# Attention and mixture of experts in one kernel: the first slot's token list on GpSimd's queue, ranks in the scores' PSUM, turns ahead of copies, the second slot turned by TensorE

## The chip, the cores and the metric

The kernel runs on one core of a Trainium2 chip. The metric is device time in microseconds (us) of one execution, the median of three runs. One more execution is recorded by the hardware profiler; its rows give the durations, and its own time stands beside its span in the table below. PE is TensorE (the matmul array), DVE VectorE, ACT ScalarE, POOL GpSimd, SP SyncE, which here only starts transfers.

## The reference

Two stages. A chunked attention (8 batches, 8 heads, 576 positions, head size 64; softmax inside each chunk of 64 positions), whose output, seen as 4608 rows of 512, goes through a mixture of experts in which each row uses one of 8 experts:

```python
scores = scale * np.matmul(q_c, k_c.transpose(0, 1, 2, 4, 3))
attn = softmax(scores)                       # within a chunk of 64
x = np.matmul(attn, v_c)                     # -> rows [4608, 512]

logits = x @ w_gate + modality_bias[modality_id]
e_idx = np.argmax(logits, axis=1)
gate_w = softmax(logits)[row, e_idx]
for e in range(8):
    mask = e_idx == e
    h = np.maximum(x[mask] @ w1[e], 0.0)     # 512 -> 1024
    out[mask] = gate_w[mask, None] * (h @ w2[e])
```

Which expert a row takes is known only when its attention is done. All is in float32; the kernel splits the operands of the expert matmuls in a high and a low part (three matmuls for one).

## The kernel before

**Attention in rounds.** A tile is 128 rows, and a round takes two; 18 rounds make the 36 tiles. In round r the code issues: `evict(r-1)` (ACT copies the attention output, L280), `parts(r-2)` (ACT copies the gate logits out of PSUM, L299) and `put(r-2)` (rows to DRAM tensor `xd`, on ACT's queue, L305), `scores(r+1)` (64 small matmuls into PSUM tile `sb`, L232; DVE takes the maxima, L235, and subtracts, L236), `transposes(r)` (PE, L257; ACT copies, L259), `rows(2r-2)`, `rows(2r-1)` (matmuls that turn the output back and form the logits, into the PSUM pairs `y0`, `y1`, L289; DVE scales, L291), `exps(r+1)` (ACT's exponential, L242; a half-sum on GpSimd, L244), `sums(r)` (DVE, L248), `values(r)` (L272). Each engine runs its own instructions strictly in the order in which the code issues them. The first 12 rounds (`NPURE`) are pure; the steps of the last six are strewn by `merge` between the matmuls of the first expert slots, where one `pair()` of PSUM holds both halves of a step.

**Routing.** Tiles form groups: `GROUPS = ((0, 8), (8, 8), (16, 20))` (first tile, count). When a group's logits are there, `route` runs as a generator, one step per `advance`: logits and argmax on GpSimd and DVE, running counts (`scan`), then two small matmuls that give each row its rank within its expert (L364, L365), taken out by DVE (L366 to L374). `scatter` then writes one 64-byte record (row number, gate) per row into a DRAM table `tab`, in which every expert has its own stretch: one indirect transfer of GpSimd's queue per tile (L380). In the pure rounds the ranks use `pairs[0]`, where `rows` writes as well.

**Slots.** A slot is 384 rows of one expert (the last two 256). Slot 0 is chosen by `early_table(0)` after group 0, slots 1 to 3 by `early_table(1)` after group 1, the others by `slot_table` after group 2. Since a list's end may be unwritten, `blank` (SP, L439) writes 384 records of a number out of range behind each of the chosen lists, or, before slot 4, behind the rows of each of the 8 experts. `locate` (SP, L559) reads a list into `tl`; it waits for the scatters and the blanks. `gather` (GpSimd) copies the row numbers (`tk`, L576 or L578) and fetches the rows into `xg` by three indirect transfers (L580). Slot 0's rows are turned by PE (`split`, L620 to L623); later slots' rows go to DRAM (`stash`), come back in blocks of 32 (`place`), are turned in blocks on DVE (`turn`, L606) and split in two parts (`part`, L611, L612).

**A slot's matmuls.** Eight steps f: `first` (12 matmuls, L679, then relu on ACT, L683, and the low part on DVE, L684), and one step later `second` (9 matmuls, L693). Weights come by `fetch` (SP, two steps' worth, 1 MB, L638) into three buffers `raw`; ACT copies the high part (L649) and DVE the low one (L653).

**What sets the order.** Two tables written by hand. `PLAN` gives, for round r and place k in it (`hook(r, k)`), what else is issued: fetches, list, gather, weight splits (`hi`, `lo`) of slot 0. `PREP` gives the same for slot s and step f; `settle` drains all open routing steps. SP's queue is in order too: a transfer that waits holds all transfers behind it.

Of the kernel before, what the change touches and what calls it, by code (L numbers as in the profile page):

```python
# [89 lines left out]
def attention_moe(ctx: ExitStack, tc: tile.TileContext, qkv, mod, cst, bias, wcat, wfst, out):  # L90
# [160 lines left out]
    def transposes(r, banks):  # L251
        ex = exs.pop(r)
        ats = []
        for j, bank in enumerate(banks):
            ap = bank.rearrange("p (k q) -> p k q", k=NP)
            for k in range(NP):
                PE.transpose(ap[:, k, :], ex[:, j * NP + k].rearrange("p u k -> p (u k)"), ident)  # L257
# [1 line left out]
            A.copy(ats[j], ap)  # L259
# [681 lines left out]
```

## Time and profile before

| | |
|---|---|
| median of 3 runs | 592.32 us (592.18 to 596.98) |
| the profiled execution | 592.26 us; its span, first to last instruction, 590.1 us |
| PE busy | 537.2 us, 91% of the span; mean granted clock 0.963 |
| DVE, ACT, POOL busy | 358.0, 240.8, 167.5 us |
| moved by DMA | 131.16 MB, mean 222 GB/s |
| first matmul of slot 0, 1, 2 | 102.94, 170.18, 220.25 us |

Busy time counts the engine's executing time; in the 40-slice strips of the page each digit is the busy share of a 14.75 us slice in tenths. A row of the timeline reads: start, duration, engine, line, operation, tiles and shapes, count; in brackets the idle time of the engine just before, and who ended it. "PEclk" is the share of full TensorE clock that was granted. Rows of SPq and ACTq are starts of transfers.

### The profile page before, as it was taken

What the parts mean: (1) busy time and instruction counts of PE and PEld (TensorE: products, weight loads), DVE (VectorE), ACT (ScalarE), POOL (GpSimd) and SP (SyncE); (2) the same over time, 40 slices, a digit from 0 to 9 for tenths busy, and PEclk for the clock granted to TensorE, in tenths of its full rate; (3) what the DMA queues carried; (4) which work ended last, traced back from release to release, by engine and by line L of the source; (5) the groups of instructions that cost most, each with busy time, mean ns of one, the idle gap of its engine ahead of it and who ended that gap; (6) DMA issues with size and microseconds to landing.
All of it is one profiled execution on the core that took longest, in us unless ns stands there. A gap on an engine that the chain in (4) does not pass through costs nothing.

```text
span 590.1 us, 12218 instructions
## 1 busy us (share of the span) xinstructions
PE 537.2 (91%) x4901; PEld 477.8 (81%) x4902; DVE 358.0 (61%) x608; ACT 240.8 (41%) x402; POOL 167.5 (28%) x171
## 2 busy tenths in 40 slices
PE   6878877996999999998699999999999999999993
PEld 3767876875877889996599998999998988998993
DVE  4659767873576597961455656555564656465741
ACT  3546354533344444431343434343443434435531
POOL 2313646113313237724222230404022110302001
PEclk9989787998899999998799999999999999999998
DMA  8989789758777727207997584867667474756500
GB/s 345 401 301 341 246 301 347 292 192 264 194 243 251 228 94 253 77 18 241 311 284 269 156 278 150 289 197 253 204 186 283 120 261 154 249 179 190 186 37 25
DMA packets 55073, 131.16 MB, mean 222 GB/s; under 512 B 11806, under 2 KB 29918, under 8 KB 46048
## 3 DMA queue, kind: packets, MB, share of 16 engines
q1 hardware_dynamic: 43040, 101.68, 52.5%
q0 software_dynamic: 7072, 19.18, 9.3%
q10 hardware_dynamic: 4896, 9.44, 4.1%
q8 instruction: 40, 0.66, 0.4%
q14 instruction: 25, 0.20, 0.1%
HBM read 102.16 MB, written 28.64 MB: 222 GB/s over the span
## 4 chain that ended last, share of the span: by engine, by line
PE 59%; issue 19%; DVE 9%; DMA 4%; ACT 3%; POOL 3%; SPq 1%; ACTq 0%; POOLq 0%; DVEq 0%
PE y L679 21%; PE sb L693 16%; PE t L693 8%; PE y L289 5%; PE t L679 3%; PE t L272 2%; PE sb L232 1%; DVE mx L235 1%; PE t L257 1%; POOL out L708 1%; DVE xr L291 1%; DVE wl L653 1%; DMA raw<-in_wfst 1%; DMA qk<-in_qkv 1%; POOL xg L580 1%
## 5 line engine op out<-in xcount | busy, mean ns | idle before, releaser
L653 DVE TENSOR_TENSOR wl<-raw,wh 128x1024 fp32r<-128x1024 f32 x104 | 127.4, 1227 | 59.4 <-ACT wh L649 59.3
L679 PE MATMUL y<-xh,wh 128*128 128x384 f32 (+1 forms) x364 | 119.6, 329 | 0.0
L679 PE MATMUL y<-xl,wh 128*128 128x384 f32 (+1 forms) x364 | 119.4, 328 | 0.0
L679 PE MATMUL y<-xh,wl 128*128 128x384 f32 (+1 forms) x364 | 119.0, 327 | 0.0
L649 ACT CAST wh<-raw 128x1024 fp32r<-128x1024 f32 x104 | 108.1, 1042 | 26.1 <-DMA raw<-in_wcat 22.1
L683 ACT ACTIVATE hh<-y 128x384 fp32r<-128x384 f32 (+1 forms) x91 | 43.1, 473 | 171.7 <-PE y L679 171.4
L684 DVE SCALAR_TENSOR_TENSOR hl<-y,hh 128x384 fp32r<-128x384 f32 (+1 forms) x91 | 48.4, 532 | 96.4 <-ACT hh L683 96.4
L708 POOL DMA_INDIRECT out<-yo,tk x37 | 39.8, 1077 | 228.0 <-DVE yo L707 199.7
L693 PE MATMUL sb<-wh,hl 128*128 128x512 f32 x208 | 84.5, 406 | 6.4 <-DVE hl L684 6.4
L693 PE MATMUL sb<-wh,hh 128*128 128x512 f32 x208 | 84.4, 406 | 1.7 <-ACT hh L683 1.7
L693 PE MATMUL sb<-wl,hh 128*128 128x512 f32 x208 | 83.1, 399 | 0.0
L679 PEld LDWEIGHTS y<-xh,wh 128*128 128x128 f32 x364 | 68.9, 189 | 3.7
L679 PEld LDWEIGHTS y<-xl,wh 128*128 128x128 f32 x364 | 68.9, 189 | 3.5
L679 PEld LDWEIGHTS y<-xh,wl 128*128 128x128 f32 x364 | 68.7, 189 | 0.0
L693 PEld LDWEIGHTS sb<-wh,hl 128*128 128x128 f32 x208 | 39.8, 192 | 17.2 <-DVE hl L684 7.8
L289 PE MATMUL y<-cs,xt 128*128 128x144 f32 x288 | 45.1, 316 | 6.5 <-DVE ra L369 5.4
L289 PEld LDWEIGHTS y<-cs,xt 128*128 128x128 f32 x288 | 42.9, 217 | 6.8 <-DVE ra L369 5.9
L244 POOL TENSOR_TENSOR sr<-ex 128x512 f32<-128x512 f32 x18 | 23.7, 1319 | 86.7 <-ACT ex L242 86.6
L580 POOL DMA_INDIRECT xg<-xd,tk x37 | 44.2, 1193 | 13.9 <-issue 7.3
L693 PEld LDWEIGHTS sb<-wh,hh 128*128 128x128 f32 x208 | 39.6, 191 | 7.5 <-ACT hh L683 2.0
L380 POOL DMA_INDIRECT tab<-tg,pi x36 | 39.3, 1091 | 20.5 <-DVE pi L374 10.9
L693 PEld LDWEIGHTS sb<-wl,hh 128*128 128x128 f32 x208 | 39.7, 191 | 5.7
(178 smaller groups left out, 707.5 us busy)
## 6 DMA issues: line engine op xcount, KB each, us to landing
raw<-in_wcat SPq DMA_DIRECT2D x48, 1024.0 KB, 6.3
qk<-in_qkv SPq DMA_DIRECT2D x18, 1024.0 KB, 7.9
v<-in_qkv SPq DMA_DIRECT2D x18, 512.0 KB, 5.9
xd<-xr ACTq DMA_DIRECT2D x18, 512.0 KB, 6.6
xs<-xg SPq DMA_DIRECT2D x10, 768.0 KB, 5.7
xq<-xs SPq DMA_DIRECT2D x40, 192.0 KB, 4.3
raw<-in_wfst SPq DMA_DIRECT2D x4, 1024.0 KB, 9.5
xs<-xg SPq DMA_DIRECT2D x2, 512.0 KB, 6.9
```

The source lines that it names most:

```text
L244: G.tensor_tensor(sring[r % 2][:, :, :, 0:32], exu[:, :, :, 0:32], exu[:, :, :, 32:64], ALU.add)
L272: PE.matmul(xps[u][hh * 64:hh * 64 + 64, p, cs_], v[us, h, c], ats[h // NP][us, h % NP, cs_], start=True, stop=True)
L289: PE.matmul(fp[:, p, 0:GWC], xt[:, p, :], gw[:, p, :], start=True, stop=True)
L380: w = G.indirect_dma_start(tab, bass.IndirectOffsetOnAxis(ap=pi[:, j:j + 1], axis=0), tg[:, j, :], None, bounds_check=E * CAP - 1, oob_is_ ...
L580: G.indirect_dma_start(xg[:, t, :], None, xd[0:n, :], bass.IndirectOffsetOnAxis(ap=tk[:, t:t + 1], axis=0), bounds_check=n - 1, oob_is_err ...
L649: A.copy(hi, raw)
L653: (G if pool else V).tensor_tensor(lo, raw, hi.bitcast(F32), ALU.subtract)
L679: PE.matmul(hp, a[:, ks], b[:, k, 0:n], start=(m == 0), stop=(m == 3 * NK - 1))
L683: A.activation(hh[:, 0:n], hp, AF.Relu)
L684: V.scalar_tensor_tensor(hl[:, 0:n], hp, 0.0, hh.bitcast(F32)[:, 0:n], ALU.max, ALU.subtract)
L693: PE.matmul(y, a[:, tsl], b[:, DM:2 * DM], start=(f == 0 and i == 0), stop=(f == NF - 1 and i == 2))
L708: w = G.indirect_dma_start(out, bass.IndirectOffsetOnAxis(ap=tk[:, t:t + 1], axis=0), yo, None, bounds_check=N - 1, oob_is_err=False)
```

## The change

- **Order of a round.** `parts` and `put` of round r-1 are issued in round r after `exps(r+1)`, instead of those of r-2 at its start; `hook(r, 1)` stands ahead of `sums(r)`.
- **Ranks.** In the pure rounds they are put into `sb[:, 0]` at place 1 of a round, after `rows`, instead of `pairs[0]` at place 0. `GATES` holds group 1's routing back to round 10 and its ranks to round 11 or later.
- **Turns ahead of copies.** `transposes` issues all eight turns, then the two copies.
- **First list.** `setup` blanks the first 384 records of each expert's stretch of `tab` once, in one transfer of ACT's queue with 1024 pieces of 192 bytes. `blank 0` goes away; `early_table(0)` no longer works out an end, and has one step less per slot. `locate 0` is issued by GpSimd, on its own queue, at round 8.
- **Weights of slot 0.** `fetch 0` moves to the start of round 8; the low parts of its first two steps are formed on GpSimd (`lop`) at rounds 10 and 11 instead of on DVE (`lo`).
- **Second slot.** Its rows are turned by PE (`split 1 0`, `split 1 2` at steps 6 and 7 of slot 0), so its weights come in the other row order (`wfst`); `stash 1`, `place 1`, `turn 1`, `part 1` go away.
- **Late tiles.** The last 20 tiles form two groups of 12 and 8. After the ranks of the last one the ends of the experts' rows are cast to `stop`, and the eight blanks before slot 4 are issued there, ahead of `slot_table`; `PREP` no longer has `blank 2`.

On GpSimd in the pure rounds: `tab` is a scatter, `sr` the half-sum of a round, `tl` slot 0's list, `xg` its rows, `lp` and `lh` routing of group 1. Before:

```order
L380 DMA tab<-tg_130,pi_1037 41472x16 x2
L320 TENSOR_TENSOR lp_140<-lp_140,ris 128x512
L244 TENSOR_TENSOR sr_142<-ex 128x16x32
L325 TENSOR_TENSOR lh<-lp_140 128x256
L326 TENSOR_TENSOR lh<-lh 128x8x16
L327 TENSOR_TENSOR lg<-lh 128x64
L328 TENSOR_TENSOR lg<-lg,mb 128x64
L244 TENSOR_TENSOR sr_143<-ex 128x16x32
L576 COPY tk_164<-tl_163 128x3
L580 DMA xg<-xd,tk_164 128x512 x3
```

The same place after the change:

```order
L394 DMA tab<-tg_131,pi_964 41472x16 x3
L247 TENSOR_TENSOR sr_147<-ex 128x16x32
L575 TENSOR_LOAD e_tab_1078
L575 ISA x2
L576 ISA
L576 DMA tl_168<-tab 128x3x2
L593 COPY tk_169<-tl_168 128x3
L597 DMA xg<-xd,tk_169 128x512 x3
L247 TENSOR_TENSOR sr_146<-ex 128x16x32
L327 TENSOR_TENSOR lp_144<-lp_144,ris 128x512
```

The list's transfer has come into GpSimd's own queue behind the last three scatters and one half-sum; the half-sum of round 10 (`sr_146`) now stands behind the list and the gather, and group 1's routing behind that.

On GpSimd in slot 0, around the second slot's gather (`tl` with its list, `tk`). Before:

```order
L380 DMA tab<-tg_133,pi_1601 41472x16 x7
L244 TENSOR_TENSOR sr_143<-ex 128x16x32
L576 COPY tk_166<-tl_165 128x3
L580 DMA xg<-xd,tk_166 128x512 x3
L244 TENSOR_TENSOR sr_142<-ex 128x16x32
```

After:

```order
L671 TENSOR_TENSOR wl_155<-raw_111,wh_154 128x1024
L247 TENSOR_TENSOR sr_146<-ex 128x16x32
L394 DMA tab<-tg_134,pi_1709 41472x16 x6
L247 TENSOR_TENSOR sr_147<-ex 128x16x32
L394 DMA tab<-tg_134,pi_1709 41472x16 x2
L247 TENSOR_TENSOR sr_146<-ex 128x16x32
L593 COPY tk_171<-tl_170 128x3
L597 DMA xg<-xd,tk_171 128x512 x3
L333 TENSOR_TENSOR lh<-lp_143 128x384
L334 TENSOR_TENSOR lh<-lh 128x12x16
```

Group 1's scatters have moved into slot 0, and the gather stands one half-sum later: that of round 14 is now ahead of it. The half-sum of round 15 comes behind the gather and four additions of group 2's routing.

On SP before slot 4 (`tab<-none` is a blank, `s_tab` the table of the late slots, `raw` a weight fetch). Before, the end of the eight blanks:

```order
L439 DMA tab<-none 128x48
L558 TENSOR_LOAD s_tab
L558 ISA x2
L559 ISA
L559 DMA tl_163<-tab 128x3x2
L638 ISA
L638 DMA raw_111<-in_wcat 128x2048
L588 DMA xs_73<-xg 128x3x512
```

After:

```order
L656 DMA raw_113<-in_wcat 128x2048
L575 TENSOR_LOAD s_tab
L575 ISA x2
L576 ISA
L576 DMA tl_168<-tab 128x3x2
L656 ISA
L656 DMA raw_111<-in_wcat 128x2048
L605 DMA xs_74<-xg 128x3x512
```

The blanks no longer stand between the fetches and the list: they have moved up to the end of slot 1, ahead of the fetch that slot 2 issues at its step 0, and wait for `stop` instead of `s_tab`.

```diff
-    9: {0: ["blank 0"], 1: ["locate 0"], 2: ["hi 0"]},
+    8: {0: ["fetch 0"], 1: ["locate 0"], 2: ["gather 0"]},
...
-        6: ["place 1", "gather 2"], 7: ["turn 1 0", "turn 1 1", "part 1 0", "part 1 1", "turn 1 2", "turn 1 3",
+        4: ["gather 1"], 5: ["locate 2", "locate 3"], 6: ["split 1 0"], 7: ["split 1 2", "gather 2"]},
...
-GROUPS = ((0, 8), (8, 8), (16, 20))
+GROUPS = ((0, 8), (8, 8), (16, 12), (28, 8))
+NSPLIT = 2
...
     def setup():
+        A.dma_start(tab[0:E * CAP, :].rearrange("(e c) r -> e c r", e=E)[:, 0:SLOT]
+                    .rearrange("e (p a) r -> p e (a r)", p=P),
+                    none.unsqueeze(1).to_broadcast([P, E, SLOT // P * ROW]))
...
-        for j, bank in enumerate(banks):
-            ap = bank.rearrange("p (k q) -> p k q", k=NP)
+        aps = [b.rearrange("p (k q) -> p k q", k=NP) for b in banks]
+        for j, ap in enumerate(aps):
             for k in range(NP):
                 PE.transpose(ap[:, k, :], ex[:, j * NP + k].rearrange("p u k -> p (u k)"), ident)
+        for j, ap in enumerate(aps):
             ats.append(ak.tile([P, NP, P], F32, name=f"at{j}", bufs=1))
             A.copy(ats[j], ap)
...
-        for _ in range(2 if g < NLEV else 5):
+        for _ in range(2):
+            yield
+        while clock[0] < go:
             yield
...
-        for _ in range(0 if g < NLEV else 3):
-            yield
...
-        jobs.append(early_table(g) if g < NLEV else slot_table())
         pooljobs.append(scatter(g, pi, tg))
+        if early:
+            jobs.append(early_table(g))
+        if last:
+            V.tensor_copy(stop, base[-1])
+            yield
+            jobs.append(slot_table())
+            blank(NLEV)
...
+        if lv == 0:
+            V.tensor_copy(rt[:, 0:2 * ne], rf[:, 0:2 * ne])
+            return
...
-        row = SP.value_load(tabs[lv][0:1, n + k:n + k + 1], min_val=0, max_val=E * CAP)
-        rd = SP.dma_start(tl, tab[ds(row, SLOT), 0:2].rearrange("(t p) c -> p t c", p=P))
+        eng = SP if s else G
+        row = eng.value_load(tabs[lv][0:1, n + k:n + k + 1], min_val=0, max_val=E * CAP)
+        rd = eng.dma_start(tl, tab[ds(row, SLOT), 0:2].rearrange("(t p) c -> p t c", p=P))
...
     def hook(r, k):
-        advance(pe=pairs[0][:, 0] if k == 0 else None)
+        clock[0] = r
+        advance(pe=sb[:, 0] if k == 1 else None)
...
     for r in range(NPURE):
         if r:
             evict(r - 1)
-        if r > 1:
-            parts(r - 2)
-            put(r - 2)
         scores(r + 1, sb)
         hook(r, 0)
         transposes(r, ts)
...
         exps(r + 1)
+        if r:
+            parts(r - 1)
+            put(r - 1)
+        hook(r, 1)
         sums(r)
-        hook(r, 1)
         values(r, ts)
```

More of the change, by code (lines that the diff above doesn't have):

```diff
@@ L316, in tl @@
             return wk.tile([P, n, E], dt, name=name, bufs=bufs)
+        early, last = g < NLEV, g == len(GROUPS) - 1
+        begin, go = GATES.get(g, (0, 0))
+        while clock[0] < begin:
+            yield
         l0 = lps[g % 2][:, 0:n]
-        (G if g < NLEV else V).tensor_tensor(
+        (G if early else V).tensor_tensor(
             l0, l0, ris[:, ts].unsqueeze(3).to_broadcast([P, n, H, E]), ALU.mult)
-        yield
+        if not early:
+            yield
         lh = wk.tile([P, n, H // 2, E], F32, name="lh", bufs=1)
@@ L382, in scatter @@
                 tg[:, j, :], None, bounds_check=E * CAP - 1, oob_is_err=True)
-            apart(w, f"tab{g}")
+            apart(w, f"tab{min(g, NLEV)}")
             marks.append(w.ins.name)
@@ L388, in attention_moe @@
     taken = cp.tile([P, E], F32, name="taken")
+    stop = cp.tile([P, E], I32, name="stop")
     def early_table(lv):
@@ L419, in early_table @@
         V.reduce_sum(rf[:, 0:2 * ne], t4, axis=AX.X)
+        rt = cp.tile([P, 3 * ne], I32, name=f"e_tab{lv}")
+        tabs[lv] = rt
+        if lv == 0:
+            V.tensor_copy(rt[:, 0:2 * ne], rf[:, 0:2 * ne])
+            return
         yield
@@ L430, in early_table @@
         V.tensor_tensor(pr, pr, far, ALU.add)
-        rt = cp.tile([P, 3 * ne], I32, name=f"e_tab{lv}")
         V.tensor_copy(rt, rf)
-        tabs[lv] = rt
     def blank(lv):
-        n, o = (LEVELS[lv][1], 2 * LEVELS[lv][1]) if lv < NLEV else (E, 2 * NREST + 1)
+        src, n, o = (tabs[lv], LEVELS[lv][1], 2 * LEVELS[lv][1]) if lv < NLEV else (stop, E, 0)
         for i in range(n):
-            row = SP.value_load(tabs[lv][0:1, o + i:o + i + 1], min_val=0, max_val=E * CAP + (NEARLY - 1) * SLOT)
+            row = SP.value_load(src[0:1, o + i:o + i + 1], min_val=0, max_val=E * CAP + (NEARLY - 1) * SLOT)
             w = SP.dma_start(tab[ds(row, SLOT), :].rearrange("(p a) c -> p (a c)", p=P), none)
@@ L449, in upto @@
     def upto(lv):
-        return sum(n for _, n in GROUPS[:lv + 1])
+        return sum(n for _, n in GROUPS[:lv + 1]) if lv < NLEV else NT
     def slot_table():
@@ L524, in slot_table @@
         yield
-        rf = t1("rf", [2 * R + 1 + E])
+        rf = t1("rf", [2 * R + 1])
         row = rf[:, R:2 * R]
@@ L547, in slot_table @@
         yield
-        rt = cp.tile([P, 2 * R + 1 + E], I32, name="s_tab")
+        rt = cp.tile([P, 2 * R + 1], I32, name="s_tab")
         V.tensor_copy(rt, rf)
@@ L556, in locate @@
         lv, k, n = where(s)
[L557 to L559 removed]
+        assert len(marks) >= upto(lv) and (ends[lv] or lv == 0)
+        eng = SP if s else G
+        row = eng.value_load(tabs[lv][0:1, n + k:n + k + 1], min_val=0, max_val=E * CAP)
+        rd = eng.dma_start(tl, tab[ds(row, SLOT), 0:2].rearrange("(t p) c -> p t c", p=P))
         after(rd, marks[:upto(lv)] + sum(ends[:lv + 1], []))
@@ L612, in part, with split @@
         V.tensor_tensor(l, x, h.bitcast(F32), ALU.subtract)
-    def split(k, bank):
-        hi, lo = (x[:, k:k + 2] for x in xring[0])
+    def split(s, k, bank=None):
+        bank = pair() if bank is None else bank
+        hi, lo = (x[:, k:k + 2] for x in xring[s])
         for i in range(2):
             for t in range(NTT):
-                assert ("rows", 0, t) in ready
+                assert ("rows", s, t) in ready
                 PE.transpose(bank[:, i, t * P:(t + 1) * P], xg[:, t, (k + i) * P:(k + i + 1) * P], ident)
@@ L637, in fetch @@
         raw = rawr[g // 2 % 3][:, f % 2:f % 2 + n]
-        SP.dma_start(raw, (wcat if s else wfst)[ds(ereg[s], 1), :, f:f + n, :].rearrange("e p f c -> p (e f) c"))
+        SP.dma_start(raw, (wfst if s < NSPLIT else wcat)[ds(ereg[s], 1), :, f:f + n, :].rearrange("e p f c -> p (e f) c"))
         for i in range(n):
@@ L758, in attention_moe @@
     merging = [True]
+    clock = [0]
     def advance(lists=None, pe=None):
@@ L789, in tick @@
             merging[0] = False
-    ahead = {"locate": locate, "gather": gather, "stash": stash, "place": place, "turn": turn, "part": part, "settle": settle,
+    ahead = {"locate": locate, "gather": gather, "stash": stash, "place": place, "turn": turn, "part": part, "settle": settle, "split": split,
              "blank": blank, "fetch": fetch, "hi": whi, "lo": wlo, "lop": lambda g: wlo(g, None, True)}
@@ L834, in attention_moe @@
             setup()
+    clock[0] = NPURE
     evict(NPURE - 1)
-    parts(NPURE - 2)
-    put(NPURE - 2)
-    split(0, sb)
-    split(2, pairs[0])
+    split(0, 0, sb)
+    split(0, 2, pairs[0])
     rows(2 * NPURE - 2, pairs[1])
```

13 lines of the change are left out of this document (7 added, 6 removed), and 13 rows, old and new, of tables (PLAN, PREP).

## The prediction

> **What bounds the kernel now.** I read the strips first, then the stretches between the marks at which slots begin, then PE's waits, then the timeline at each wait.
>
> ```profile
> PE   6878877996999999998699999999999999999993
> PEclk9989787998899999998799999999999999999998
> ...
> 0.00:102.94 102.94, 78.38 (x1908) 70.42 (x1909) 70.49 (x152) 46.90 (x90) 44.16 (x56) 0.90 0.89 326
> 102.94:170.18 67.24, 58.92 (x771) 49.93 (x769) 40.85 (x74) 25.71 (x46) 14.56 (x14) 0.95 0.73 241
> 170.18:220.25 50.07, 47.07 (x425) 40.71 (x426) 35.80 (x59) 23.83 (x43) 15.24 (x13) 1.00 0.59 195
> 220.25:300.54 80.29, 72.24 (x340) 63.81 (x339) 49.45 (x105) 27.60 (x42) 37.23 (x34) 0.94 0.56 180
> 300.54:590.10 289.56, 280.56 (x1464) 252.96 (x1463) 161.45 (x223) 116.74 (x183) 56.27 (x54) 0.99 0.61 197
> ```
>
> The columns after the length are the busy times of PE, PE's weight loads, DVE, ACT and POOL, then PE's granted clock, the DMA share and GB/s. From 300 us on PE is full: nothing here touches that. Before it, PE idles 24.6 us in the pure rounds (A), 8.3 in slot 0 (B), 3.0 in slot 1 (C), 8.05 in slots 2 and 3 (D), and the clock is down besides. The waits with a name:
>
> ```profile
> PE sb L693 <- DVE hl L684: 6.4, 2, 5.7
> PE y L289 <- DVE ra L369: 5.4, 2, 3.2
> PE y L257 <- ACT at L259: 5.4, 6, 1.3
> PE y L257 <- ACT lp L299: 4.6, 2, 4.1
> PE t L257 <- ACT xt L280: 3.1, 1, 3.1
> ```
>
> (total, times, longest). That is 24.9 us of PE's own time, and each of the long ones costs more than its length:
>
> ```profile
> 45.69 2.13 PE L289 MATMUL y<-cs,xt 128*128 128x144 f32 x16
> ...
> 59.81 4.21 PE L289 MATMUL y<-cs,xt 128*128 128x144 f32 x16 [2.29 <-DVE ra L369]
> ...
> 93.89 4.21 PE L289 MATMUL y<-cs,xt 128*128 128x144 f32 x16 [3.16 <-DVE ra L369]
> ```
>
> The same 16 matmuls take 4.21 us instead of 2.13 after an idle of 2.29 us: the clock is halved for a while. I charge a wait above 2 us with some 2 us more. [...]
>
> **A, the pure rounds.**
>
> ```profile
> 44.90 1.23 DVE L235 TENSOR_REDUCE mx<-sb 128x16 f32<-128x1024 f32 x1 [0.40 <-PE sb L232]
> 49.91 1.23 DVE L235 TENSOR_REDUCE mx<-sb 128x16 f32<-128x1024 f32 x1 [0.40 <-PE sb L232]
> 60.77 1.19 POOL L380 DMA_INDIRECT tab<-tg,pi  x1 [5.86 <-DVE pi L374]
> L380 POOL DMA_INDIRECT tab<-tg,pi x36 | 39.3, 1091 | 20.5 <-DVE pi L374 10.9 <-issue 9.6
> tab<-tg,pi POOLq DMA_INDIRECT x36, 4.2
> tl<-tab SPq DMA_DIRECT2D x13, 3.0 KB, 4.0
> xg<-xd,tk POOLq DMA_INDIRECT x37, 5.4
> L620 PE MATMUL sb<-cs,xg 128*128 128x128 f32 x6 | 0.9, 282 | 0.0
> L623 DVE TENSOR_TENSOR xl<-sb,xh 128x768 fp32r<-128x768 f32 x1 | 1.0, 951 | 0.0
> L364 PE MATMUL y<-oh,ub 128*128 128x64 bf16 x2 | 0.4, 190 | 0.7 <-ACT lp L299 0.7
> tab<-none SPq DMA_DIRECT2D x12, 24.0 KB, 1.5
> 7.50:15.00 7.50, 4.40 (x148) 3.33 (x147) 5.47 (x6) 3.63 (x6) 1.64 (x2) 1.00 1.02 411
> ```
>
> An undisturbed round is 5.01 us (44.90 to 49.91), of which DVE works 4.6. Out go: both rank waits, 5.4 us, with a halved clock behind each (2.1), so 9.6; and ACT's wait for slot 0's weights, behind which `xt` stands (3.1, with a cold stretch 5.1), because `fetch 0` starts over a round earlier. PE alone would then begin slot 0 at 102.94 - 14.7 = 88.2. Moving `parts` and `put` costs nothing: ACT has room in a round, and the logits come a round earlier.
>
> In comes a chain on GpSimd. Group 0's ranks move up a round, but now wait until DVE has emptied `sb`; I put the first scatter at 57.5 instead of 60.77. Then, in queue order: 8 scatters at 1.09 + 0.27 = 10.9, two half-sums at 1.27 (row below, L244) 2.5, to 71; the last scatter lands 4.2 after its start, 74; the list is issued (1.1, as a scatter) and lands in 4.0 (SP's own lists) to 5.4 (GpSimd's gathers), taken as 4, to 79; three gathers 4.1, to 83; their rows land 5.4 after the last start, 87. All the while nothing else runs on GpSimd: the half-sum of round 10 is queued behind (84.5), DVE's `sums(10)` waits for it in order, and behind that stand a round's DVE work (4.6), 15 small routing instructions (0.17 each, row L413 below, 2.6) and `split`'s two subtractions (0.95 each, 1.9): 93.6. The rows alone would let PE start at 87 + 0.9 + 0.9 + a copy = 90. So slot 0 begins between 88.2 and 94; I take **93**, by the DVE queue, which has the most behind it. The early blank, 1024 small pieces in the place of 128, costs at most 8 x 1.5 = 12 of transfers and at least nothing (it only adds traffic, so no gain); it lies some 40 us ahead of the chain, which has the rounds between to take it up, so I charge nothing and keep 2 for the range. DMA sets a floor that decides nothing: 326 GB/s for 102.94 us, moved at the 411 of the fullest stretch, is 81.7.
>
> **B and C, slots 0 and 1.** The longest wait of slot 0 is a queue, read from GpSimd to PE:
>
> ```profile
> 135.41 0.19 POOL L576 COPY tk<-tl 128x3 int32<-128x3 int32 x1 [15.29 <-DMA tl<-tab]
> ...
> 140.67 1.27 POOL L244 TENSOR_TENSOR sr<-ex 128x512 f32<-128x512 f32 x1
> ...
> 141.97 0.70 DVE L248 TENSOR_REDUCE sm<-sr 128x16 f32<-128x528 f32 x1 [4.89 <-POOL sr L244]
> ...
> 143.54 0.21 ACT L299 COPY lp<-y 128x64 f32<-128x64 f32 x1 [7.72 <-DVE xr L291]
> ...
> 143.81 0.76 PE L257 MATMUL y<-cs,ex 128*128 128x128 f32 x4 [4.14 <-ACT lp L299]
> ...
> 119.10 1.04 DVE L424 TENSOR_TENSOR ef<-ef,elim 128x3 f32<-128x3 f32 x1
> L413 DVE TENSOR_TENSOR taken<-taken,etn 128x8 f32<-128x8 f32 x4 | 0.7, 167 | 0.1
> ```
>
> GpSimd waits 15.29 us for the second slot's list, the half-sum queues behind, then DVE, ACT, PE. The change puts this half-sum ahead of the gather, so 4.14 + 2 go. The six waits on `at` go with the turns (5.4: four in slot 0, 3.6; two in slot 1, 1.8). In come in slot 0: twelve turns of the second slot, 0.9 + 0.9, two rank matmuls, 0.4 (row L364); and on DVE, between the first step and the turns of round 13, the ranks of group 1 (6 instructions) and one more pass of the table (10), 16 x 0.17 = 2.7, which must pass before PE may use the bank. PE comes there 0.8 earlier, DVE 2 later: a wait of 0.5 (4.6 less the 4.14) grows to about 3, with the cold clock 4.5 more than before. The half-sum of round 15 now queues behind the gather; if the list lands no later than before, counted from slot 0's start, that costs about 1. GpSimd's low parts, 2 x 1.27 each by the half-sum's row, lie before slot 0 and hide in A. B: 67.24 - 3.6 - 6.1 + 2.2 + 4.5 + 1 - 2 = 63, where the last 2 are what is left of the 8.3 of idle and of the clock's 0.05 x 67.24 (the cold stretch after the 4.14, small waits). Bounds: 57 without DVE's wait, 68 with a list 5 later. C: 50.07 - 1.8 - 1 (waits for the parts, which DVE now has done) = 47.3; between 46 and 50, since slot 1 takes over group 3's routing.
>
> A small DVE instruction took 1.04 instead of 0.17 (L424) while a half-sum ran on GpSimd. [...]
>
> **D, slots 2 and 3.**
>
> ```profile
> 255.70 8.18 SPq L439 DMA_DIRECT2D tab<-none  x8
> 265.57 0.41 SPq L559 DMA_DIRECT2D tl<-tab  x1
> 266.18 0.35 SPq L638 DMA_DIRECT2D raw<-in_wcat  x1
> ...
> 271.24 1.04 ACT L649 CAST wh<-raw 128x1024 fp32r<-128x1024 f32 x1 [8.09 <-DMA raw<-in_wcat]
> ...
> 284.67 0.58 DVE L606 STREAM_TRANSPOSE xq<-xq 128x384 f32<-128x384 f32 x1 [9.53 <-DMA xq<-xs]
> ...
> 285.75 0.80 PE L693 MATMUL sb<-wh,hl 128*128 128x512 f32 x1 [5.75 <-DVE hl L684]
> ```
>
> SP holds eight blanks until 263.9, the list and the weights stand behind them; ACT waits 8.09 for the weights, DVE 9.53 for the turned rows, and PE for `hl` behind that. Idle 8.05 and the clock's 0.06 x 80.29 = 4.8 make 12.9. After the change the blanks pass at the end of slot 1, only 8 scatters (10.9) instead of 20 (27) follow the last ranks, and the table has six steps less to wait for: the list is read some 10 us earlier, which is more than the 9.53 that DVE waited. What is late next is the fetch behind the eight blanks: its buffer has two steps more to spare than those 8.2 us take, I charge nothing and keep 4 for the range. D: 80.29 - 12.9 + 0.2 = 67.6.
>
> **Sum.** 93 + 63 + 47.3 + 67.6 + 289.6 = 560.5 of span. The profiled execution took 592.26 with 590.1 of span, so 2.2 lie around it, and it agrees with the median shown (592.32): **563**. Own range, from the bounds of A, B and C: 552 to 572.
>
> **The rivals.**
>
> *The GpSimd queue gets later still.* Every us that the first list is late beyond my 79 is a us of slot 0's start, and the second list, whose scatters now begin in slot 0, is late in turn and brings back the 4.14 with its clock. For it: 15.29 us of waiting in just this place. A at 99, B at 68: 574, between 572 and 588.
>
> *The chain binds nothing.* GpSimd's half-sum has slack of a round, slot 0 begins at 88.2, and DVE keeps up in slot 0 (58): 553, down to 545. Against it: the queue order on GpSimd leaves sums no other place.
>
> *The idle time only changes its name.* The rounds are held by loads (DMA share 0.89 over A, above 1 in the fullest stretch), so A stays at 100; B keeps 67, and slots 2 and 3 wait 8 for the fetch behind the blanks (76 and no better): 100 + 67 + 47.3 + 76 + 289.6 + 2.2 = 582 with all of it, 588 with the rank waits back on `sb`.
>
> *Slower.* One list on a blocked queue can eat everything: GpSimd in order holds half-sums, DVE and PE. It decides from the point at which the first list lands 36 us later than 79, at 115, since the change is worth 30: then slot 0 starts at 129 and the time is 599. Against it: the longest wait for a list in the trace is the 15.29 above.
>
> **How the numbers follow.** A measurement of this kernel can tell about 1% from no change, so the bounds are 586.4 and 598.2. Forecast 0.66; later queue 0.17, of which 0.01 lies above 586; nothing binds 0.10; same idle time 0.04, most of it just inside 1%; slower 0.03. Predicted 563. From 549 to 578 holds the forecast, two thirds of the faster case and half of the later queue: 0.8. Faster 0.92, same 0.05, slower 0.03.
>
> **What would show it.** In the profile after: no wait of `y` L289 on `ra`, none of `y` L257 on `at`; slot 0's first matmul near 93, with DVE's `sm` waiting for `sr` shortly before; slots 0 and 1 about 63 and 47 long; no wait of SP on `s_tab` with blanks behind it, and 67 from slot 2 to slot 4. Wrong it is if `sr` never waits behind the first list, if the turns of round 13 don't wait for DVE, or if `raw` stops ACT in slot 2.

## The result and the profile after

The changed kernel takes 573.38 us (median of four runs, 572.34 to 575.57), the kernel before 592.25 beside it: a ratio of 0.968, 95% interval 0.961 to 0.975. So it is 18.9 us faster, where 29 were forecast. The profiled execution took 572.34 with 570.6 of span. Ratios and intervals, here and below, leave out executions that as a whole ran slower at a lower granted clock (of before on chip 2, six at 615.0 to 618.9 us and 0.942 to 0.948 beside six at 603.9 to 609.5 and 0.955 to 0.962), and one of the experiment turns_mixed at 1812.9 us; medians are over all.

The strips of the page after the change, its DMA strip, and then the same five stretches between the marks at which slots begin (length; busy PE, weight loads, DVE, ACT, POOL; PE's granted clock, DMA share, GB/s):

```profile
PE   6859776879899999999999999999999999999994
PEclk9888989899999999999999999999999999999998
DMA  8997999536939706869784866748586573656400
...
0.00:104.69 104.69, 77.37 (x1905) 68.55 (x1907) 71.15 (x127) 48.58 (x90) 44.03 (x56) 0.90 0.92 343
104.69:167.80 63.11, 57.18 (x786) 49.63 (x786) 50.24 (x110) 27.98 (x48) 24.34 (x24) 1.00 0.55 188
167.80:214.20 46.40, 46.03 (x433) 40.81 (x428) 32.85 (x62) 21.20 (x39) 29.54 (x27) 1.00 0.59 188
214.20:281.50 67.30, 67.30 (x338) 60.58 (x337) 46.00 (x93) 27.97 (x42) 20.42 (x20) 1.00 0.76 249
281.50:570.60 289.10, 280.67 (x1465) 253.01 (x1463) 161.57 (x223) 116.79 (x183) 58.73 (x54) 0.99 0.60 195
```

| stretch | before | forecast | after |
|---|---|---|---|
| A, pure rounds | 102.94 | 93 | 104.69 |
| B, slot 0 | 67.24 | 63 | 63.11 |
| C, slot 1 | 50.07 | 47.3 | 46.40 |
| D, slots 2 and 3 | 80.29 | 67.6 | 67.30 |
| E, the rest | 289.56 | 289.6 | 289.10 |

(D of before ends at 300.54, as the prediction cuts it; slot 4's first matmul begins at 300.38.) From slot 0 on the forecast is met within 1 us everywhere. The whole miss lies in the pure rounds: they were to become 10 shorter and are 1.75 longer. PE's waits after the change (total, times, longest) show what took the place of those on `ra` and `at` and of the long one on `hl`:

```profile
PE sb L235 <- issue: 8.1, 3, 3.6
PE y L638 <- ACT lp L302: 7.5, 2, 4.7
PE t L260 <- ACT xt L283: 4.5, 4, 1.7
```

The longest with a name, 4.7 us for `lp`, ends A. Its chain is read backwards on four engines, from the timelines between 92 and 102 us (start, duration; in brackets the idle time before and who ended it; `wl` are the low parts, `sr` the half-sums):

```profile
101.32 1.54 PE L638 MATMUL y<-cs,xg 128*128 128x128 f32 x6 [4.67 <-ACT lp L302]
...
101.06 0.21 ACT L302 COPY lp<-y 128x64 f32<-128x64 f32 x1 [6.38 <-DVE xr L294]
...
93.69 2.05 DVE L343 TENSOR_TENSOR lg<-lg,gmx 128x64 f32<-128x64 f32 x1
95.77 1.19 DVE L345 SCALAR_TENSOR_TENSOR va<-lg,cs 128x64 f32<-128x64 f32 x1
96.99 0.22 DVE L347 TENSOR_REDUCE fm<-va 128x8 f32<-128x64 f32 x1
97.25 2.01 DVE L350 TENSOR_TENSOR oh<-va,fm 128x64 bf16<-128x64 f32 x1
99.29 1.13 DVE L351 COPY scan<-oh 128x64 bf16<-128x64 bf16 x1
100.34 1.28 DVE L294 TENSOR_TENSOR xr<-y,ris 128x512 f32<-128x512 f32 x2
...
93.30 2.36 POOL L671 TENSOR_TENSOR wl<-raw,wh 128x1024 fp32r<-128x1024 f32 x1
95.61 1.27 POOL L247 TENSOR_TENSOR sr<-ex 128x512 f32<-128x512 f32 x1
96.83 2.35 POOL L671 TENSOR_TENSOR wl<-raw,wh 128x1024 fp32r<-128x1024 f32 x1
99.13 1.26 POOL L247 TENSOR_TENSOR sr<-ex 128x512 f32<-128x512 f32 x1
```

PE's second turned bank waits for `lp`, `lp` for `xr`, and `xr` stands on DVE behind five routing steps of group 1. Four of these steps take 1.13 to 2.05 us, and each ends within 0.1 us of the end of an instruction on GpSimd: 95.74 beside 95.66, 96.96 beside 96.88, 99.26 beside 99.18, 100.42 beside 100.39. The fifth, a reduction (L347), takes its usual 0.22. GpSimd was at work without a break here, with the two low parts that the change gave it.

The other end of A is early. SP's waits in the first 50 us, its timeline, and three single microseconds of the stretch view:

```profile
SPq L118 <- DMA tab<-none: 9.0, 1, 9.0
...
17.89 0.33 SPq L113 DMA_DIRECT2D qk<-in_qkv  x1
27.29 0.33 SPq L118 DMA_DIRECT2D v<-in_qkv  x1
...
26.00:27.00 1.00, 1.00 (x30) 0.85 (x28) 1.00 (x3) 0.68 (x1) 0.00 (x0) 1.00 0.45 148
27.00:28.00 1.00, 0.56 (x36) 0.42 (x32) 1.00 (x2) 0.69 (x3) 0.55 (x1) 1.00 0.18 70
28.00:29.00 1.00, 1.00 (x83) 1.00 (x77) 0.34 (x2) 0.50 (x2) 0.73 (x1) 1.00 0.95 94
```

A load of `v` waits 9.0 us for the early blank, which was issued at 13.66, though it takes nothing from it; why it waits for it the trace does not show. It left at 27.29; the same load left at 22.64 before. DMA, busy for 0.92 of A on average, then moved 70 to 148 GB/s for three microseconds. The scores of round 6 began at 47.45 instead of 43.72.

### The profile page after: what moved, and what is told of

Its sections match the earlier page's. It is cut to its first block, busy times and chain, and to the rows that moved or that the text cites. A ratio compares the mean times of both kernels' runs of the same rounds, so it can differ in the third digit from the quotient of the medians.

```text
span 570.6 us, 12242 instructions
## 1 busy us (share of the span) xinstructions
PE 528.6 (93%) x4915; PEld 472.6 (83%) x4916; DVE 361.8 (63%) x611; ACT 242.5 (43%) x401; POOL 177.1 (31%) x180
## 3 DMA queue, kind: packets, MB, share of 16 engines
q10 hardware_dynamic: 5936, 9.64, 4.8%
## 4 chain that ended last, share of the span: by engine, by line
PE 63%; issue 19%; DVE 8%; POOL 5%; DMA 2%; ACT 2%; SPq 0%; POOLq 0%; ACTq 0%; DVEq 0%
PE y L697 25%; PE sb L711 18%; PE t L711 9%; PE y L292 3%; PE t L697 3%; DVE wl L671 2%; PE sb L235 1%; POOL out L726 1%; POOL xg L597 1%; PE t L260 1%; DMA tab<-tg,pi 1%; PE t L275 1%; POOL tab L394 1%; DMA qk<-in_qkv 1%; DVE mx L238 1%
## 5 line engine op out<-in xcount | busy, mean ns | idle before, releaser
L711 PE MATMUL sb<-wh,hl 128*128 128x512 f32 x208 | 82.3, 396 | 0.0
L394 POOL DMA_INDIRECT tab<-tg,pi x36 | 40.2, 1117 | 39.0 <-DVE pi L382 11.8
L292 PE MATMUL y<-cs,xt 128*128 128x144 f32 x288 | 43.2, 307 | 2.2 <-issue 2.2
L292 PEld LDWEIGHTS y<-cs,xt 128*128 128x128 f32 x288 | 41.2, 209 | 1.1 <-ACT xt L283 0.8
```

The source lines that it names most:

```text
L292: PE.matmul(fp[:, p, 0:GWC], xt[:, p, :], gw[:, p, :], start=True, stop=True)
L394: w = G.indirect_dma_start(tab, bass.IndirectOffsetOnAxis(ap=pi[:, j:j + 1], axis=0), tg[:, j, :], None, bounds_check=E * CAP - 1, oob_is_ ...
L711: PE.matmul(y, a[:, tsl], b[:, DM:2 * DM], start=(f == 0 and i == 0), stop=(f == NF - 1 and i == 2))
```

## The experiments

Theory L: DVE's routing steps are held by GpSimd. Theory P: the blank's 1024 pieces hold SP. Theory Q is the prediction's: the list's way through GpSimd's queue sets slot 0's start. The runs fell on three more chips. On chip 3 (before: 590.6 us) times agree with the first measurement; on chips 2 and 4 before takes 612.2 and 619.5. So times are compared only within a chip, or as ratios to before; the unedited change was run only on the first chip and on chip 3 (control). The stretch lengths are read from each run's trace.

| run | chip | time | ratio to before, interval | A | B | C | D |
|---|---|---|---|---|---|---|---|
| few_pieces | 2 | 586.89 | 0.965, 0.962 to 0.969 | 103.80 | 71.40 | 52.36 | 67.29 |
| low_on_dve | 2 | 584.69 | 0.963, 0.959 to 0.967 | 103.19 | 70.68 | 52.28 | 67.24 |
| gate_late | 2 | 580.91 | 0.957, 0.953 to 0.960 | 100.60 | 71.67 | 53.26 | 67.24 |
| one_group | 2 | 581.87 | 0.959, 0.955 to 0.964 | 105.79 | 66.46 | 46.90 | 71.29 |
| control | 3 | 574.06 | 0.970, 0.965 to 0.976 | 103.99 | 64.83 | 46.39 | 67.57 |
| both8 | 3 | 567.71 | 0.962, 0.955 to 0.970 | 92.21 | 71.21 | 46.37 | 67.22 |
| blanks_late | 3 | 572.91 | 0.971, 0.965 to 0.977 | 104.73 | 63.09 | 46.37 | 67.24 |
| slot1_by_dve | 3 | 577.03 | 0.975, 0.970 to 0.980 | 102.04 | 68.36 | 48.05 | 68.04 |
| both8_spread | 4 | 580.96 | 0.944, 0.938 to 0.949 | 99.43 | 73.56 | 52.01 | 67.25 |
| few8 | 4 | 585.89 | 0.953, 0.946 to 0.961 | 103.03 | 71.85 | 52.05 | 67.23 |
| turns_mixed | 4 | 595.66 | 0.968, 0.958 to 0.978 | 106.75 | 73.99 | 56.82 | 67.43 |
| list_on_sp | 4 | 585.09 | 0.950, 0.942 to 0.958 | 104.57 | 68.83 | 52.53 | 68.02 |

### The changed kernel as its own yardstick: control

No edit.

> The changed kernel itself, as the yardstick of the runs beside it, since this chip may differ from the one of the first measurement: 0.968 of before. By stretches: slot 0 begins at 104.7 to 106, slots 0 and 1 together 109.5 on the first chip and 113 to 124 on the second (where groups of 64 by 64 matmuls stop for 0.4 us every few instructions), slots 2 and 3 67.3.

A at 103.99 and a ratio that agrees with the first. Over the runs that leave both suspected causes in, A lies between 102.0 (slot1_by_dve) and 106.8 (turns_mixed): a difference of 2 in A from a single run says little.

### The early blank in fewer pieces: few_pieces and few8

The blank's source is a tile of 16 partitions (8 in few8) instead of 128, and its destination is cut to match.

```
...
-                    none.unsqueeze(1).to_broadcast([P, E, SLOT // P * ROW]))
+                    none16.unsqueeze(1).to_broadcast([16, E, SLOT // 16 * ROW]))
```

> Edit: the early blank writes the same 192 KB in 128 pieces of 1536 B from 16 partitions, in the place of 1024 pieces of 192 B from 128; all else as in the changed kernel. Theory P (pieces): SP's load of v for round 4 stood 9.0 us until the blank's 1024 small pieces had landed, and DMA then moved only 70 to 148 GB/s from 26 to 29 us. With 128 pieces that wait goes (under 2 us is left), v and qk go out near 23 us and not 27.3, the score block of round 6 starts near 44 and not 47.45, and all behind it moves up with it: slot 0's first matmul near 101 instead of 104.69, the time 573.4 - 3.7 = 570. Theory Q (my prediction's: the blank costs nothing, and the queue list, gather, half-sum on GpSimd alone sets slot 0's start): within 1 us of 573.4, since the rounds before the list have the slack to take it up. Theory I (instruction loading by chance): the gap in the middle of the scores of round 5 (3.60 us) stays whatever the blank does, and slot 0's start moves by less than 1.5.

> Edit: only the early blank in 64 pieces in the place of 1024. On another chip 128 pieces cut SP's wait for the blank from 9.0 to 4.2 us, the scores of round 6 began at 41.75 against 45 to 47.5, and slot 0 at 103.8 against 105.8, with the 3.9 us for lp behind the locked DVE steps still there. If the two causes add, the blank alone is worth 5 to 7 of the 11.8 us that both gave together: slot 0 at 97 to 99, the time 5 to 7 below that of the changed kernel (0.96 of before). If they add only together (the early gain is eaten at the locked steps), slot 0 at 101 to 103 and the time 1 to 3 below.

With 128 pieces the wait for the blank falls to 4.2 us, with 64 to 3.9. The load leaves at 22.61 and 22.47, as before the change, and DMA moves 412 to 453 GB/s where it had moved 70 to 148. In the runs with the old blank the scores of round 6 began at 46.1 on average (44.6 to 47.6, nine traces), with the new one at 43.1 (41.8 to 44.9, four traces). So the mechanism of theory P is shown, worth some 3 us there on average. But slot 0 began at 103.80 and 103.03, only 1.5 to 2 us earlier than with the old blank on the same chips (one_group 105.79, list_on_sp 104.57), not at 101 or 97 to 99. In few_pieces PE still waits 3.95 for `lp` at the end. In few8 it does not wait for `lp` there at all: DVE came to the routing steps while GpSimd stood idle, and they took their usual time (DVE, then GpSimd; list_on_sp shows the same):

```profile
98.16 0.22 DVE L345 TENSOR_TENSOR lg<-lg,gmx 128x64 f32<-128x64 f32 x1
98.94 0.22 DVE L352 TENSOR_TENSOR oh<-va,fm 128x64 bf16<-128x64 f32 x1
...
99.23 1.28 POOL L249 TENSOR_TENSOR sr<-ex 128x512 f32<-128x512 f32 x1 [1.07 <-ACT ex L247]
```

Both runs lose time earlier, in PE itself. From the score maxima of round 8 to those of round 9, beside the eight scatters of group 0, few_pieces needs 10.6 us (few8 11.0):

```profile
59.06 1.22 DVE L240 TENSOR_REDUCE mx<-sb 128x16 f32<-128x1024 f32 x1
...
69.64 1.22 DVE L240 TENSOR_REDUCE mx<-sb 128x16 f32<-128x1024 f32 x1 [5.42 <-PE sb L237]
```

It is 10.0 to 11.0 in all eight traces of chips 2 and 4, and 5.1 in the five traces of the change and its edits on the first chip and chip 3. PE's small matmuls stop there again and again (last section). So what an edit gains early in A can be lost on these two chips before slot 0 begins. Theory I, stalls by chance, is not ruled out either: the stop in the middle of round 5's scores stayed, 2.78 and 3.88.

### The lock-out on DVE: low_on_dve and gate_late

```
...
-    10: {0: ["lop 0"], 2: ["hi 1"]},
-    11: {0: ["lop 1", "fetch 2"], 2: ["fetch 4"]},
+    10: {0: ["lo 0"], 2: ["hi 1"]},
+    11: {0: ["lo 1", "fetch 2"], 2: ["fetch 4"]},
```

> Edit: the low parts of slot 0's first two weight halves go back from GpSimd to DVE, at the same places of the order (rounds 10 and 11). Theory L (lock-out): in the last pure round five of DVE's routing steps of group 1 took 6.9 us in the place of 1.3, each ending as an instruction on GpSimd ended, and round 10's xr, behind them on DVE, held lp and PE's second turned bank by 4.67 us. Without the two low parts on GpSimd (2.36 us each) only the half-sums (1.27) still hold DVE: the five steps take some 3 us, DVE does 2 x 1.25 more, PE's wait for lp falls from 4.67 to about 2, slot 0's first matmul comes at 102 instead of 104.69, the time is about 571. Theory Q (the GpSimd queue sets it by the list and the half-sums): the half-sum of round 11 still follows the gather, so xr does not move: 573.4, or 1 to 2 slower for the 2.5 us more on DVE, which is the fullest engine of a round.

In the timeline of low_on_dve (DVE, then GpSimd) two of the four steps are back at their own length (L345; L351 with 0.18), and the other two each end with a half-sum:

```profile
95.77 0.98 DVE L343 TENSOR_TENSOR lg<-lg,gmx 128x64 f32<-128x64 f32 x1
96.78 0.23 DVE L345 SCALAR_TENSOR_TENSOR va<-lg,cs 128x64 f32<-128x64 f32 x1
...
97.30 0.93 DVE L350 TENSOR_TENSOR oh<-va,fm 128x64 bf16<-128x64 f32 x1
...
95.39 1.28 POOL L247 TENSOR_TENSOR sr<-ex 128x512 f32<-128x512 f32 x1
96.84 1.31 POOL L247 TENSOR_TENSOR sr<-ex 128x512 f32<-128x512 f32 x1 [0.17 <-ACT ex L245]
```

L343 ends at 96.75 and the half-sum at 96.67, L350 at 98.23 and the half-sum at 98.15. The wait for `lp` is 2.1 (expected 2; 4.9 in one_group on the same chip) and A 103.19, 2.6 below one_group. Theory L's sizes came out; theory Q had 0 to +2. The 2.6 alone is little more than A varies; the wait is the surer sign.

```
-GATES = {1: (10, 11)}
+GATES = {1: (10, 12)}
...
-   ... 1: ["hi 4", "lo 4", "hi 5", "lo 5"], 3: ...
+   ... 1: ["hi 4", "lo 4", "hi 5", "lo 5", "step", "step", "step"], 3: ...
```

A "step" advances the second table by one part.

> Edit: the part of group 1's routing that DVE does is held back until the rounds are over and goes into slot 0's first two steps (three extra steps of the table in step 1, so that the second slot's expert is known when its weights are fetched). GpSimd keeps list, gather, low parts and half-sums as they are. Theory L: nothing small stands ahead of round 10's xr any more; xr follows right behind ex at 93.5, lp at 95, PE's 4.67 us for lp and the cold clock behind it go, and slot 0 begins at 99 to 100.5 instead of 104.69, now by the gathered rows (landed at 96). In slot 0 some 4 us of DVE come back in front of hl, so slot 0 is 63.1 to 66 long; the time 568 to 572. Theory Q: slot 0's start waits for GpSimd's half-sum of round 11, so it stays at 103 to 105, and the time is 573 to 576 with the steps added to slot 0.

DVE's timeline of gate_late shows `xr` right behind `ex`:

```profile
94.44 1.22 DVE L239 TENSOR_TENSOR ex<-sb,mx 128x1024 f32<-128x1024 f32 x1
95.58 1.34 DVE L294 TENSOR_TENSOR xr<-y,ris 128x512 f32<-128x512 f32 x2
```

The wait for `lp` at the end of A is gone, slot 0 begins at 100.60, 5.2 before one_group. Theory Q (103 to 105) falls: list, gather and half-sums were left as they were.

What the traces show of the hold on DVE: after the change, beside GpSimd's instructions, L343 and L350 took 2.05 and 2.01, the reduction L347 0.22; in few8, with GpSimd idle, the same two steps (L345, L352 there) took 0.22. Through what GpSimd holds DVE is not shown.

### Both causes away: both8

The edits of few8 and gate_late together.

> Both causes away at once: the early blank in 64 pieces of 3 KB (from 8 partitions) and DVE's part of group 1's routing behind the rounds. If the blank's wait on SP (theory P) and the lock-out with its queue on DVE (theory L) are separate terms of the 11.7 us that slot 0 is later than I forecast, their gains add: slot 0 begins 6 to 8 us earlier than in the control, at 97 to 99.5, slots 0 and 1 grow by at most 2, and the time is 4 to 7 below the control. If one of them hides the other (theory Q: the list's way through GpSimd decides, since the list is read when its scatters have landed), slot 0 begins no more than 5 us earlier than in the control, as with the late routing alone (100.6 against 105.8).

The stretches of both8, its SP and PE waits, and the matmuls behind the wait:

```profile
0.00:92.21 92.21, 72.12 (x1907) 63.95 (x1907) 62.74 (x113) 47.30 (x89) 41.43 (x56) 0.96 0.95 353
92.21:163.42 71.21, 62.20 (x787) 54.75 (x785) 53.73 (x124) 28.85 (x49) 27.81 (x26) 0.90 0.59 214
...
SPq L118 <- DMA tab<-none: 3.4, 1, 3.4
...
PE t L699 <- DVE hl L704: 4.3, 2, 4.2
...
116.48 0.69 PE L699 MATMUL t<-xh,wh 128*128 128x384 f32 x1 [4.15 <-DVE hl L704]
```

Slot 0 begins at 92.21, where the prediction had 93, and 11.8 before the control on the same chip: more than the 6 to 8 expected, and than the single gains of 2 and 5.2 on chip 2 added up. The traces show where chip 2 falls behind: up to the score maxima of round 8 both8 (59.13) and few_pieces (59.06) run alike, and those of round 9 follow at 64.20 here and at 69.64 there. So the single gains of chip 2 are no measure for chip 3; how the 11.8 divides between the two causes stays open. The first list had landed by 79.3 (forecast 79, after 84.2). Of the 11.8, B gives back 6.4: PE waits 4.15 for `hl`, behind table steps that this edit itself had pressed into one step, and the next 12 matmuls take 4.2 us instead of 2.35 (the granted clock of B is 0.90, 0.97 in the control). The time is 6.3 below the control.

### The table steps spread: both8_spread

Against both8:

```
...
-        if f % 2 == 0 and g + 6 < end:
+        if f % 2 == 0 and g + 6 < end and g + 6 != NF:
...
-   ... 1: ["hi 4", "lo 4", "hi 5", "lo 5", "step", "step", "step"], 3: ...
+   ... 1: ["hi 4", "lo 4", "hi 5", "lo 5"], 2: ["step", "fetch 8"], 3: ...
```

> With both causes away slot 0 began at 92.2 (control 104.0), but slot 0 was 71.2 long (64.8): PE waited 4.15 us for hl, behind some 30 small steps of the second table on DVE that my own edit had pressed into one step, and the next 12 matmuls took 4.2 us instead of 2.35. Edit: the fetch of slot 1's first weights comes one step of slot 0 later, so that these table steps are spread over two steps of slot 0. Theory: what slot 0 gave back was this order on DVE alone; slot 0 at 65 to 67, slot 0's start still at 92 to 93, the time 4 to 6 below the 567.7 of the run before it, 562 to 564 where before takes 590.6 (0.953 of before). Rival: DVE is full in slot 0's first 22 us whatever the order, and the work only waits elsewhere (behind lp or the second slot's bank): slot 0 stays at 69 to 72 and the time at 566 to 569.

The wait for `hl` goes, 4.3 to 0.2, so the order on DVE was its cause. The length of slot 0 can't be compared with both8's: it fell on chip 4, where B and C together are 121 to 131 long in every run, against 109.5 and 111.2 of the changed kernel on the first chip and chip 3. Against few8 on that chip A is 3.6 shorter, B 1.7 longer and the time 4.9 lower. PE waits 3.6 for `lp` ahead of the second slot's first bank (2.0 in few8, 2.8 in both8), as the rival has it; whether slot 0 is shorter for the spreading is not shown. Its ratio, 0.944, is the lowest of all, and the changed kernel's was 0.968 and 0.970; but list_on_sp, whose edit takes away neither cause, has 0.950 on this chip, so most of that distance is the chip's.

### The list on SP: list_on_sp

```
-        eng = SP if s else G
+        eng = SP
```

> Edit: the first slot's list is read on SP's queue, at the same place of the order. On GpSimd it was issued at 78.8, 4.8 us after GpSimd's last instruction, when its eight scatters had landed. On SP the same wait stands ahead of the loads of v and qk of rounds 11 and 12 (issued at 73.0 and 76.5) and of slot 0's weights. Theory: these loads leave 2 to 6 us later, a round waits for them, and slot 0 begins 2 to 5 later than 104 to 105 (time 575 to 580 on the first chip's scale, 0.971 to 0.98 of before). Rival: the loads run some two rounds ahead of their use and take it up; GpSimd's list (0.8 us to issue, 5.4 to land) then only changes its queue, and slot 0 begins within 1 us, or 1 to 2 earlier.

The list is issued at 76.73 and has landed by 83.0; GpSimd's was issued at 78.8 and had landed by 84.2 (after the change, first chip). A is 104.57: the rival's "within 1 us", and the 2 to 5 of the theory are not there. But on this chip PE was late by its own stops: from 90 us to slot 0 it waited neither for the gathered rows nor for `lp`. So the list had room here, and the run does not tell what its queue is worth on the first chip.

### Turns and copies mixed again: turns_mixed

```
         for j, ap in enumerate(aps):
             for k in range(NP):
                 PE.transpose(ap[:, k, :], ex[:, j * NP + k].rearrange("p u k -> p (u k)"), ident)
-        for j, ap in enumerate(aps):
             ats.append(ak.tile([P, NP, P], F32, name=f"at{j}", bufs=1))
             A.copy(ats[j], ap)
```

> Edit: the copy of the first bank of a round's turns goes back between the turns of the first and of the second bank, as before the change. By my account the waits of PE on at, 5.4 us in six places of slots 0 and 1, come back in this order: slots 0 and 1 together 3.5 to 5.5 longer than 109.5 to 111.2. Rival: the order of the two copies on ACT is the same with and without the edit (nothing stands between them), so the compiled order does not change and neither does the time (within 1 of the changed kernel); then what took the waits away was something else, such as the place of exps or sums behind the turns.

PE's waits in this run:

```profile
PE y L260 <- ACT at L262: 8.3, 5, 5.0
```

The waits on `at` are back, and B and C are 130.8 long, against 121.4 to 125.6 in the other runs on that chip. One of the five waits is 5.0 long, at a place where ACT itself came late; the other four are 3.3 together, about 0.8 each as before the change. So the rival, that nothing changes, falls, and the account's 0.9 for one wait holds. The price of the order alone can't be read from B and C here: the long wait is in it, and its cause was not followed up.

### The second slot turned by DVE again: slot1_by_dve

```
-NSPLIT = 2
+NSPLIT = 1
...
-        4: ["gather 1"], 5: ["locate 2", "locate 3"], 6: ["split 1 0"], 7: ["split 1 2", "gather 2"]},
+        4: ["gather 1"], 5: ["locate 2", "locate 3", "stash 1"], 6: ["place 1", "gather 2"], 7: ["turn 1 0", "turn 1 1", "part 1 0", "part 1 1", "turn 1 2", "turn 1 3",
+                                       "part 1 2", "part 1 3"]},
```

> Edit: the second slot is again turned over DRAM and DVE (written out, read back in blocks, 4 turns and 8 parts), as before the change; all else stays. List 1 is read at some 140, its rows have landed near 152; the write and the four reads add some 5.5 and 4, the turns and parts some 4 on DVE and ACT: the second slot's input is complete near 168, just when slot 1 would begin, where PE's own turns have it at 167.4. Theory: the turns by PE pay only the way over DRAM; slots 0 and 1 together become 2 to 6 longer than in the control, with a wait of PE for xl or xq at the start of slot 1. Rival (PE is full in slot 0, and its 12 turns, 1.8 us, and the 2.8 us wait for their bank go): the same or up to 4 faster.

PE's waits from 92 to 220 us:

```profile
PE t L698 <- ACT xh L629: 7.9, 1, 7.9
```

PE waits 7.9 us for the parts of the second slot, and B and C are 116.4 long against the control's 111.2: 5.2 more, inside the theory's 2 to 6. The turns by PE save the way over DRAM.

### The late tiles in one group: one_group

```
-GROUPS = ((0, 8), (8, 8), (16, 12), (28, 8))
+GROUPS = ((0, 8), (8, 8), (16, 20))
```

> Edit: the last two groups of tiles are one again, of 20 tiles; the blanks stay where the change put them, at the end of slot 1. By my account of slots 2 and 3 (the ranks of the last 8 tiles come early and only 8 scatters follow them, the blanks no longer stand ahead of the list): with one group 20 scatters (27 us) follow the last ranks, the list for slot 4 is read some 10 us later or more, and slots 2 and 3 take 72 to 80 instead of 67.3 with a wait of PE for hl behind DVE's turns: 578 to 586. Rival: the blanks' place alone was worth it; then slots 2 and 3 stay at 67 to 69 and the time within 2 us of 573.4.

GpSimd's last scatter and SP's list for slot 4:

```profile
252.05 0.98 POOL L394 DMA_INDIRECT tab<-tg,pi  x1 [0.30 <-issue]
...
254.47 0.39 SPq L576 DMA_DIRECT2D tl<-tab  x1
```

The list goes out 35.3 us after slot 2's start (219.15), 29.6 in the changed kernel (243.77 less 214.20). D is 71.29, 4.0 longer than in the three other runs on the chip: less than the 5 to 13 expected, but not nothing, as the rival had it. The table of the late slots, which the list reads, is done 34.3 us after slot 2's start, and 28.6 in the changed kernel. B and C are 113.4 long, 9.6 to 11.6 shorter than in the other three; the last section comes back to this.

### The blanks behind the table: blanks_late

```
             jobs.append(slot_table())
-            blank(NLEV)
...
-        6: ["part 3 2", "turn 3 3"], 7: ["part 3 3", "settle", "locate 4", "gather 4"]},
+        6: ["part 3 2", "turn 3 3"], 7: ["part 3 3", "settle", "blank 2", "locate 4", "gather 4"]},
```

> Edit: the eight blanks of the last level go back behind the table of slots, ahead of the list for slot 4, as they stood before the change; the two groups of late tiles stay. With one group and the blanks early, slots 2 and 3 took 71.3 against 67.3. By my account of slots 2 and 3 the rest of the 13 us (80.3 to 67.3) hangs on the blanks: SP holds 8.2 us ahead of the list and of the weights, so ACT waits for raw and PE for hl again: slots 2 and 3 at 72 to 76, the time 5 to 9 above the control. Rival: with the ranks of the last 8 tiles early, the table is ready early enough that 8.2 us more are hidden; then 67 to 68 and no more than 1 above the control.

SP's queue in slot 2, and the table of the late slots on DVE:

```profile
230.85 8.51 SPq L455 DMA_DIRECT2D tab<-none  x8
240.96 0.41 SPq L575 DMA_DIRECT2D tl<-tab  x1
...
239.41 0.14 DVE L564 CAST s_tab<-rf 128x41 int32<-128x41 f32 x1
```

The eight blanks hold SP for 8.5 us, yet the list goes out at 240.96, 2.8 earlier than after the change, and D is 67.24. The rival's outcome holds: the blanks' place is free. But the edit put back only the place. The blanks still take their rows from `stop` and pass while DVE works on the table. Before the change they took them from `s_tab` and could not start until it was there:

```profile
254.76 0.19 DVE L549 CAST s_tab<-rf 128x49 int32<-128x49 f32 x1
```

Then came the eight blanks (255.70 to 263.87) and only then the list (265.57): 10.8 us after the table, against 1.5 here and 1.1 in the changed kernel. That wait on the table is what this run leaves out.

## Why the prediction was right and where it was wrong

- **A, the early blank.** "I charge nothing and keep 2": this step failed. The cost was put on the transfers, which later rounds would take up; it came through a wait. A load on SP stood 9.0 us for the blank, though it takes nothing from it. It was worth 3 us at round 6 on average of the runs.
- **A, the chain on GpSimd and DVE.** "15 small routing instructions (0.17 each" failed with "GpSimd's low parts ... hide in A". In order, round 10's `xr` did stand behind the routing on DVE, as forecast, but five of these steps took 6.6 us between 93.69 and 100.42, since the low parts and half-sums on GpSimd held them. The prediction had seen 1.04 instead of 0.17 in such a place (L424 of before, which ends at 120.14, a half-sum at 120.11) and charged nothing for it. With both terms out A is 92.21, and the working holds as far as round 10's half-sum: list at 79.3 (forecast 79), gathers to 84.0 (83), half-sum to 85.3 (84.5). Its end does not: from 85.7 on PE works without a pause, and slot 0 begins before `split`'s first subtraction (92.97), which the forecast had ahead of it. So 92.21 beside 93 is luck in part.
- **B.** 63 forecast, 63.11 measured, from other parts. The wait of round 13's turns, which was to grow from 0.5 to about 3 and to cost 4.5 with its clock (before, the 16 matmuls behind each rank wait ran at a granted clock of 0.50, the undisturbed ones at 45.69 at 1.00), stayed at 0.51. In its place PE waits 1.35 and 1.11 for `hl`, and 2.82 for `lp` at 156.69, ahead of the second slot's first bank. Errors of opposite sign fell together, so the match is luck.
- **The six `at` waits.** They went, and came back when this part alone was undone, at about 0.8 each but for one of 5.0.
- **C and D.** 47.3 and 67.6 forecast, 46.40 and 67.30 measured. D's size was right, and the list for slot 4 is read 15.7 us earlier, counted from slot 2's start (45.3 before, 29.6 after; some 10 forecast). The traces split this in two: the table is done 6.1 earlier (34.7, 28.6), and the list follows it by 1.1 instead of 10.8, since the blanks no longer wait for the table. One group alone gives back 5.7 of the first part and 4.0 of D's 13. That the remaining 9 belong to the second part is argued from these times; no run undid it alone.
- **The signs.** As forecast, `sm` waits for `sr` (2.35, at 90.2) behind the first list, the waits on `ra` and `at` are gone, B, C and D have their lengths, and no blank stands behind `s_tab`; slot 0's start near 93 did not come. Two signs of being wrong came: the turns of round 13 hardly wait, and `raw` stops ACT in slot 2 twice for 3.60 us. The second costs nothing: PE is busy for all of D's 67.30.
- **The rivals.** The time fell where the first rival put it (574). A part of its mechanism is there: the list landed 5.2 late, some 3 to 3.7 of it inherited from the blank. But with list, gather and half-sums left as they were, taking routing off DVE alone gave 5.2, so these 5.2 did not hang on the list's way through GpSimd.

## What to carry to other kernels

A transfer may be waited for by one that takes nothing from it: here a load of `v` waited 9.0 us for a blank in 1024 pieces, 4.2 with 128 and 3.9 with 64. So count the pieces, and see in the waits of the other queues who stands behind it. Before work is moved to GpSimd, look which steps on DVE will run beside it and what is queued behind these steps; here four steps took 1.13 to 2.05 us beside GpSimd's instructions, two of them 0.22 with GpSimd idle, while a reduction (0.22) and a step with one input in PSUM (gate_late's `xr`, 1.34 for two beside a low part) were not held. When a stretch matches its forecast, check the parts: B did by errors of opposite sign. And when an experiment puts a transfer back, put back what it waits for too, or its place alone is tested.
